# Attention and token-mixing MLP on one core: a new written order for the first two batches, another conversion of the float64 weights, and fp32r in more of group 0's second layer

## The chip, the core and the metric

The kernel runs on one core of a Trainium2 chip. The metric is device time in microseconds (us) of one execution; lower is better. Engines are named as the profile names them: PE is TensorE (matmuls; PEld its weight loads), DVE is VectorE, ACT is ScalarE, POOL is GpSimd, SP issues the DMAs.

## What is computed

Eight batches, eight heads, 576 tokens of 64 values; the attention features are an exponential of a projection, with the largest magnitude of a row taken off. Its output is the input of a block that mixes tokens through two thin matrices and then applies a two-layer MLP. U, V and the two MLP weights come in float64.

```python
def phi(x):
    proj = np.einsum('bhsd,df->bhsf', x, w_phi)
    proj = proj - np.max(np.abs(proj), axis=-1, keepdims=True)
    return np.concatenate([np.exp(proj), np.exp(-proj)], axis=-1)
q_p, k_p = phi(q), phi(k)
kv = np.einsum('bhsf,bhsd->bhfd', k_p, v)
num = np.einsum('bhsf,bhfd->bhsd', q_p, kv)
den = np.einsum('bhsf,bhf->bhs', q_p, np.sum(k_p, axis=2))[..., None] + 1e-06
x = heads side by side of num / den              # (8, 576, 512)
u = x + (x.transpose(0, 2, 1) @ U @ V).transpose(0, 2, 1)
out = u + np.maximum(u @ w_ch1, 0.0) @ w_ch2     # 512 -> 2048 -> 512
```

## The kernel before

**Tiling.** Attention goes by pairs of heads, four pairs a batch. The MLP goes by groups of 512 tokens: a batch gives one group (512 of its 576 tokens), and the 64 tokens left over from each of the eight batches make a ninth. A group takes the 2048 hidden features in 16 tiles f of 128. `hidden(f)` is 12 matmuls of 512 columns into one PSUM bank: the layer-1 weights and the transposed input `uT` are each split into an fp32r high part and a low part, and three of the four products are taken. `relu(f)` moves the result to SBUF, and `add(f)` multiplies it with layer-2 weights into four banks `o`.

**Group 0 is special.** In its `add` the input and the weights are plain fp32: 4 matmuls for a tile (each shows as two records in the trace), with `h` written by one ScalarE `Relu` (L1090) and the converted weight `w_r` used as it is. From group 1 on, `h` is split into `h_hi` (ScalarE, L1095) and `h_lo` (VectorE, L1096) and the weights into `w_hi` and `w_lo`: 12 fp32r matmuls for a tile. The weights of layer 2 are split in `split_w2` (ScalarE L385, VectorE L386), called from group 1's `hidden`.

**Conversion.** `convert` turns a float64 tile (two 32-bit words for a number) into fp32 by integer work: `low` (ScalarE, L227) rounds the low word's upper half, `mask` (VectorE, L231) cuts out the exponent, `size` (ScalarE, L236) rescales it, `shift` is two VectorE instructions (L240, then L243 for the sign bit), and `join` (VectorE, L248) adds the two halves. 32 weight tiles go through it, and four small ones of U and V, which are then rounded and split on VectorE (L292 to L295, L317, L319).

**Order.** The first two batches (`early`) are recorded as numbered steps, each with an engine, and issued in the order of the table `ORDER` written in the file; every engine runs its own steps in that order. A word `*n` puts n filler matmuls on zeros (`busy`) into PE's queue. The table covers the attention of batches 0 and 1, the mixing of batch 0 and the first chunks of group 0's MLP; the parts behind a `/` are issued between the later chunks. From there on a fixed loop (`ordered`) interleaves the MLP of group g with the attention of later pairs.

**Three stages** are used below. Stage 1 runs up to the transposes of batch 0's `u` (L1058), behind which group 0's MLP starts; stage 2 from there to the same transposes of batch 1; stage 3 is one more batch. After it all batches are alike.

Of the kernel before, what the change touches and what calls it, by code (L numbers as in the profile page):

```python
# [1394 lines left out]
```

## Time and profile before

| what | us |
|---|---|
| median of 3 runs | 1145.04 (1143.74 to 1145.18) |
| the profiled execution: its own time | 1143.57 |
| the profiled execution: its span, first to last instruction | 1141.4 |
| PE busy in the span | 1120.8 (98%) |
| VectorE busy in the span | 655.2 (57%) |
| ScalarE busy in the span | 533.2 (47%) |
| stage 1 | 0 to 69.2 |
| stage 2 | 69.2 to 203.3 |
| stage 3 | 203.3 to 330.3 |

The table reads from the top: 98% of the span is PE at work, and the chain of work that ended last is 90% PE, 8% VectorE. Those are averages over stages with different limits, so the stages are read one by one. A PE that is busy in this profile is not always a PE at its peak, since the ends of matmuls are modelled; starts are the safer measure.

### The profile page before, as it was taken

To read this page: it belongs to the slowest core of one execution; us is meant where nothing else is said; L and a number is where in the kernel's file an instruction comes from. 1 tells how busy PE (TensorE), PEld (TensorE's weight loads), DVE (VectorE), ACT (ScalarE), POOL (GpSimd) and SP (SyncE) were. 2 spreads that over 40 slices of the span, in tenths; PEclk is the share of its full clock that TensorE was granted. 3 is DMA by queue.
4 is the path that set the end of the run, shared out by engine and by line. 5 is a ranking of instruction groups with operands and counts; after the bars stand their busy time and mean duration, and the time that the engine had idled before them with its cause. 6 is when DMAs were issued, how large, how long until landed. Compare 5 with 4: busy or idle time off the path is not lost.

```text
span 1141.4 us, 22298 instructions
## 1 busy us (share of the span) xinstructions
PE 1120.8 (98%) x9210; PEld 917.4 (80%) x9217; DVE 655.2 (57%) x1379; ACT 533.2 (47%) x1158; POOL 157.9 (14%) x119
## 2 busy tenths in 40 slices
PE   7889999999999999999999999999999999999998
PEld 5765666688888888888888888888888888888886
DVE  7999988856655656655565655665565633112111
ACT  6888876445534544354534553454544521111110
POOL 4321211011111111011201111111101110000000
PEclk9999999999999999999999999999999999999999
DMA  6355534211122112211131122211121005001001
GB/s 197 88 164 181 167 101 128 103 32 32 52 89 62 32 33 76 88 37 32 51 109 33 32 60 67 75 41 34 58 100 32 20 1 171 1 1 37 1 1 37
DMA packets 90532, 75.73 MB, mean 66 GB/s; under 512 B 51648, under 2 KB 76736, under 8 KB 90304
## 3 DMA queue, kind: packets, MB, share of 16 engines
q1 hardware_dynamic: 90112, 73.79, 21.1%
q8 instruction: 73, 1.20, 0.4%
q10 hardware_dynamic: 320, 0.52, 0.1%
q14 instruction: 27, 0.22, 0.1%
HBM read 55.41 MB, written 18.87 MB: 65 GB/s over the span
## 4 chain that ended last, share of the span: by engine, by line
PE 90%; DVE 8%; DMA 1%; SPq 0%; issue 0%; ACT 0%; DVEq 0%
PE o L1110 35%; PE ph L1079 33%; PE xp L877 5%; PE kv_ps L850 4%; PE pk L810 2%; PE T L732 2%; PE pp L969 1%; PE pt L1058 1%; PE kv_ps L840 1%; PE pq L831 1%; PE pq L832 1%; PE xp L870 1%; PE vp L993 1%; DMA w<-in_moe_w_ch_dram 1%; DVE kp L761 1%; DVE w_r L243 1%
## 5 line engine op out<-in xcount | busy, mean ns | idle before, releaser
L1079 PE MATMUL ph<-uT_hi,w_hi 128*128 128x512 f32 x576 | 231.0, 401 | 0.0
L1096 DVE SCALAR_TENSOR_TENSOR h_lo<-ph,h_hi 128x512 fp32r<-128x512 f32 x128 | 88.4, 690 | 247.4 <-ACT h_hi L1095 247.3
L1079 PE MATMUL ph<-uT_hi,w_lo 128*128 128x512 f32 x576 | 224.9, 390 | 0.0
L1079 PE MATMUL ph<-uT_lo,w_hi 128*128 128x512 f32 x576 | 224.7, 390 | 0.0
L1110 PE MATMUL o<-w_hi,h_hi 128*128 128x512 f32 x512 | 205.4, 401 | 0.0
L1095 ACT ACTIVATE h_hi<-ph 128x512 fp32r<-128x512 f32 x128 | 76.7, 599 | 266.3 <-PE ph L1079 266.2
L1110 PE MATMUL o<-w_lo,h_hi 128*128 128x512 f32 x512 | 200.2, 391 | 0.0
L1110 PE MATMUL o<-w_hi,h_lo 128*128 128x512 f32 x512 | 199.8, 390 | 0.0
L1079 PEld LDWEIGHTS ph<-uT_hi,w_lo 128*128 128x128 f32 x576 | 108.1, 188 | 23.8 <-DVE w_lo L364 0.4
L1079 PEld LDWEIGHTS ph<-uT_hi,w_hi 128*128 128x128 f32 x576 | 108.3, 188 | 22.2 <-issue 0.5
L1079 PEld LDWEIGHTS ph<-uT_lo,w_hi 128*128 128x128 f32 x576 | 108.4, 188 | 21.5 <-issue 1.0
L1110 PEld LDWEIGHTS o<-w_hi,h_lo 128*128 128x128 f32 x512 | 96.1, 188 | 21.1
L1110 PEld LDWEIGHTS o<-w_hi,h_hi 128*128 128x128 f32 x512 | 96.3, 188 | 18.8
L1110 PEld LDWEIGHTS o<-w_lo,h_hi 128*128 128x128 f32 x512 | 96.4, 188 | 17.2
L788 POOL PARTITION_ALL_REDUCE qp_t<-qp_t x24 | 17.8, 741 | 624.1 <-ACT qp_t L787 624.1
L788 POOL PARTITION_ALL_REDUCE qp<-qp x48 | 96.0, 1999 | 32.1 <-ACT qp L787 30.5
L471 DVE TENSOR_TENSOR T<-T,T 64x512 fp32r<-64x512 f32 x96 | 66.2, 689 | 33.4 <-ACT T L468 30.5
L468 ACT CAST T<-T 64x512 fp32r<-64x512 f32 x96 | 55.9, 582 | 28.8 <-PE T L732 15.6
L877 PE MATMUL xp<-kv,qp 128*64 128x65 f32 x2048 | 66.8, 222 | 1.9 <-DVE kv L857 1.5
L877 PEld LDWEIGHTS xp<-kv,qp 128*64 128x64 f32 x2048 | 63.1, 138 | 4.1 <-ACT kp L651 2.0
L850 PE MATMUL kv_ps<-vb,kp 128*64 128x65 f32 x2048 | 65.2, 221 | 0.0
L850 PEld LDWEIGHTS kv_ps<-vb,kp 128*64 128x64 f32 x2048 | 64.2, 138 | 0.0
(158 smaller groups left out, 1567.9 us busy)
## 6 DMA issues: line engine op xcount, KB each, us to landing
w<-in_moe_w_ch_dram SPq DMA_DIRECT2D x32, 512.0 KB, 3.9
raw<-in_q_dram SPq DMA_DIRECT2D x32, 256.0 KB, 2.7
raw<-in_k_dram SPq DMA_DIRECT2D x32, 256.0 KB, 2.9
vb<-in_v_dram SPq DMA_DIRECT2D x64, 128.0 KB, 2.9
u_dram<-x SPq DMA_DIRECT2D x32, 256.0 KB, 2.6
st<-u_dram SPq DMA_DIRECT2D x16, 512.0 KB, 3.8
out_dram<-st SPq DMA_DIRECT2D x32, 256.0 KB, 2.5
t_r<-in_k_dram SPq DMA_DIRECT2D x32, 32.0 KB, 2.1
```

Of the source, the lines that this page charges most:

```text
L243: nc.vector.scalar_tensor_tensor(out=a(), in0=st()[:, :, 1], scalar=-0x80000000, in1=a(), op0=ALU.bitwise_and, op1=ALU.bitwise_or)
L468: nc.scalar.copy(out=dst[0:D], in_=src)
L471: nc.vector.tensor_sub(dst[D:2 * D], src, f32(dst[0:D]))
L732: nc.tensor.transpose(out=pT[:, c * P:(c + 1) * P], in_=self.raw[n][:, c // 2, c % 2, :], identity=ident)
L788: nc.gpsimd.partition_all_reduce(qp[0], qp[1], P, ReduceOp.absmax)
L810: nc.tensor.matmul(pk[:, i, :, :], self.T[0][:, i, cs], w_hl, start=True, stop=True)
L850: nc.tensor.matmul(self.kv_v[z * HP:(z + 1) * HP, f, g, :], kp[f][:, i, z * HP:(z + 1) * HP], self.vb[:, g, t, :], start=False, stop=(t == ...
L877: nc.tensor.matmul(xv[zs, c, :], qp[f][:, c * P + z * HP:c * P + (z + 1) * HP], self.kv[:, f, c // 2, :], start=(f == 0), stop=(f == 1), s ...
L1079: nc.tensor.matmul(ph, l[:, c * P:(c + 1) * P], r[:, c, :], start=(n == 0), stop=(n == len(terms) * NCC - 1))
L1095: nc.scalar.activation(out=h_hi, in_=ph, func=AF.Relu)
L1096: nc.vector.scalar_tensor_tensor(out=h_lo, in0=ph, scalar=0.0, in1=f32(h_hi), op0=ALU.max, op1=ALU.subtract)
L1110: nc.tensor.matmul(self.o[t], l[:, cs], r, start=(f == 0 and n == 0), stop=(f == NFC - 1 and n == len(terms) - 1))
```

## The change

The conversion gets other steps. The upper word is read as fp32 and scaled by 2^-112 on ScalarE (`upper`), then shifted left by 3 as a whole on VectorE (`shift`, one instruction in place); the sign is cut out by `sign`, and `mask`, `size` and the second instruction of `shift` go. For the first eight weight tiles and for U and V the low word is done on VectorE (`low_dve`), otherwise on ScalarE as before. Rounding and copying of U and V move to ScalarE. Group 0's second layer uses the split from its third tile on (f of 2 and more): its weights are split right after conversion, its `h_lo` is made on VectorE, and `add` takes 12 fp32r matmuls instead of 4 fp32 ones. Steps become finer: the largest magnitude of k and its subtraction are two steps, and so are the denominator, its reciprocal and the products. The table `ORDER` is another one (845 numbers in place of 727), with 15 filler matmuls instead of 33.

```diff
-1 4 *8 5o 6 49 2 0 511 3 48 47 515 *1 7a 8 11oo 28ao 31 13 18 32 9o 512 10 46 54a *2 12a 52a
+4 58 1 *8 5o 6 2 *1 7o 8 0 11ao 563 13 28oo 565 32 57 33 18 63a 64 3 9a 10 38 *2 66a 77 55
...
-    def convert(work, st, a, b_, after, n, free):
+    def convert(work, st, a, b_, after, n, free, dve=False):
...
-        def mask():
+        def low_dve():
             nc.vector.tensor_scalar(
-                out=half(1), in0=words()[:, :, 3], scalar1=0x7FF0, scalar2=None,
+                out=b_().bitcast(F32), in0=words()[:, :, 1], scalar1=2.0 ** -13,
+                scalar2=2.0 ** 23, op0=ALU.mult, op1=ALU.add)
+
+        def upper():
+            nc.scalar.activation(
+                out=a().bitcast(F32), in_=st().bitcast(F32)[:, :, 1], func=AF.Copy,
+                scale=2.0 ** -112)
+
+        def sign():
+            nc.vector.tensor_scalar(
+                out=half(1), in0=words()[:, :, 3], scalar1=0x8000, scalar2=None,
                 op0=ALU.bitwise_and)
-
-        def size():
-            nc.scalar.activation(
-                out=half(1), in_=half(1), func=AF.Relu, scale=8.0, bias=e_bias)
 
         def shift():
             nc.vector.tensor_scalar(
-                out=a(), in0=st()[:, :, 1], scalar1=3, scalar2=0x7FFFF8,
-                op0=ALU.logical_shift_left, op1=ALU.bitwise_and)
-            nc.vector.scalar_tensor_tensor(
-                out=a(), in0=st()[:, :, 1], scalar=-0x80000000, in1=a(),
-                op0=ALU.bitwise_and, op1=ALU.bitwise_or)
+                out=a(), in0=a(), scalar1=3, scalar2=None, op0=ALU.logical_shift_left)
...
-            nc.vector.tensor_copy(out=u_all[pr, to, 0, :], in_=u_f[pr, of])
...
+            hi = work.add("ACT", lambda n=n: u_hi(n), (ju, zero), free=(su,))
+            last.append(work.add(
+                "DVE", lambda n=n: u_lo(n), (hi,), free=(su,)))
             for i in (2, 3):
-                nc.vector.tensor_copy(out=u_all[pr, to, i, :], in_=f32(u_all[pr, to, 0, :]))
...
+                last.append(work.add(
+                    "ACT", lambda n=n, i=i: u_copy(n, i), (ju, zero), free=(su,)))
...
-            done.append(work.add("DVE", v_part, (jv,), free=(sv,)))
+            hi = work.add("ACT", v_hi, (jv,), free=(sv,))
+            done.append(work.add("DVE", v_lo, (hi,), free=(sv,)))
...
+            elif f >= LATE:
+                hi = work.add("ACT", lambda f=f: split_w2_hi(f), (j,))
+                j = work.add(
+                    "DVE", lambda f=f: split_w2_lo(f),
+                    (hi, ready[2, f - 1] if f > LATE else None))
...
-                ks = {"t": add("DVE", lambda: k_sub("t"), (Kt,), (s_kt,), (slt,))}
...
+                    km = add(
+                        "DVE", lambda r=r: k_max(r), (Kt if r == "t" else K,),
+                        (s_m, s_kt if r == "t" else s_k[r]))
                     ks[r] = add(
-                        "DVE", lambda r=r: k_sub(r), (K, *([ks[0]] if r else [])),
-                        (s_k[r],), (sls[r],))
+                        "DVE", lambda r=r: k_sub(r), (km,),
+                        free=(s_m, slt if r == "t" else sls[r]))
...
-            if self.g == 1:
-                split_w2(f)
+            if self.g == 1 and f in w_t:
+                split_w2_hi(f)
+                split_w2_lo(f)
...
-            if self.g == 0:
+            if self.g == 0 and f < LATE:
...
-            if self.g == 0:
-                terms = ((terms, w_t[f]),)
+            if self.g == 0 and f < LATE:
+                terms = ((self.h[f], w_t[f]),)
+            else:
+                (h_hi, h_lo), w_hi, w_lo = self.h[f], w_hi_t[2, f], w_lo_t[2, f]
+                terms = ((h_hi, w_hi), (h_hi, w_lo), (h_lo, w_hi))
...
+                if f >= LATE:
+                    s_l[f] = Slot("h_lo")
+                    relu[f] = w.add(
+                        "DVE", (lambda f=f: m.relu_lo(f, got["ph", f])),
+                        (relu[f],), (s_l[f],), (sl,))
```

VectorE in stage 1, where U has been converted (`u_st` is the staged U, `u_all` its rounded copies, `qp` and `kp` features of a pair, `kv` the product of k and v). Before:

```order
L248 ISA u_st<-u_st 128x320
L634 TENSOR_TENSOR qp_0_11_191<-qp_0_11_191,qp_0_10_190 128x512
L290 MEMSET u_all 128x256
L292 CAST u_all<-u_st 128x4x32
L293 TENSOR_TENSOR u_all<-u_st,u_all 128x4x32
L295 CAST u_all<-u_all 128x4x32 x2
L292 CAST u_all<-u_st 64x32
L293 TENSOR_TENSOR u_all<-u_st,u_all 64x32
L295 CAST u_all<-u_all 64x32 x2
```

Of the change, the place where the low parts of U stand on VectorE:

```order
L918 COPY kv_2_745<-kv_ps_2_696 128x260
L233 TENSOR_SCALAR v_st_658<-v_st_658 128x256
L669 TENSOR_TENSOR qp_3_01_664<-qp_3_01_664,qp_3_00_663 128x512
L307 TENSOR_TENSOR u_all<-u_st,u_all 64x32
L307 TENSOR_TENSOR u_all<-u_st,u_all 128x4x32
L1095 TENSOR_TENSOR xs_0_2_739<-x_110,xs_0_2_739 128x256
```

The casts have left VectorE's queue, and the low parts stand among the steps of pairs 2 and 3 instead of pair 0.

VectorE in stage 2, around the weights of tiles 4 to 8 (`w_b` and `w_r` are the two halves of a conversion, `w_lo` a low part). Before:

```order
L240 TENSOR_SCALAR w_r_5_1662<-w_5_1540 128x512
L243 SCALAR_TENSOR_TENSOR w_r_5_1662<-w_5_1540,w_r_5_1662 128x512
L231 TENSOR_SCALAR w_b_7_1671<-w_7_1665 128x512
L248 ISA w_r_3_1557<-w_r_3_1557,w_b_3_1514 128x1024
L248 ISA w_r_4_1560<-w_r_4_1560,w_b_4_1538 128x1024
```

Of the change, ahead of tile 5's `add`:

```order
L248 TENSOR_SCALAR w_r_12_1779<-w_r_12_1779 128x512
L390 TENSOR_TENSOR w_lo_6_1806<-w_r_6_1604,w_hi_6_1801 128x512
L1176 SCALAR_TENSOR_TENSOR h_lo_5_1835<-ph_5_1808,h_hi_5_1821 128x512
L390 TENSOR_TENSOR w_lo_7_1849<-w_r_7_1479,w_hi_7_1847 128x512
L248 TENSOR_SCALAR w_r_8_1706<-w_r_8_1706 128x512
L243 TENSOR_SCALAR w_b_11_1858<-w_11_1764 128x512
L252 ISA w_r_8_1706<-w_r_8_1706,w_b_8_1772 128x1024
L243 TENSOR_SCALAR w_b_6_1856<-w_6_1713 128x512
L421 TENSOR_TENSOR w_lo_5_1875<-w_r_5_1624,w_hi_5_1793 128x512
```

The two-input instruction of the shift is gone; `h_lo` of tile 5 and the low part of its layer-2 weight now stand in the same queue as the conversions of tiles 8 to 12, and tile 5's `add` needs both.

PE in stage 2, the `add` of tile 3 (`o` are the four output banks). Before:

```order
L596 MATMUL pq_1_2_1669<-T_2_1339,w_f 128x512
L601 MATMUL pqt_2_1706<-tail_T_2_1338,w_f 128x128
L1110 MATMUL o_0_1437<-w_r_3_1557,h_3_1609 128x512
L1110 MATMUL o_1_1438<-w_r_3_1557,h_3_1609 128x512
L1110 MATMUL o_2_1439<-w_r_3_1557,h_3_1609 128x512
L1110 MATMUL o_3_1440<-w_r_3_1557,h_3_1609 128x512
```

Of the change, the first bank of the same `add`:

```order
L631 MATMUL pq_1_2_1679<-T_2_1336,w_f 128x512
L1191 MATMUL o_0_1410<-w_hi_3_1645,h_hi_3_1601 128x512
L1191 MATMUL o_0_1410<-w_lo_3_1681,h_hi_3_1601 128x512
L1191 MATMUL o_0_1410<-w_hi_3_1645,h_lo_3_1617 128x512
L1191 MATMUL o_1_1411<-w_hi_3_1645,h_hi_3_1601 128x512
```

Four matmuls with the converted weight became twelve with its two parts; what stands around them is almost the same.

## Rows read from the trace of the kernel before

**Rows 1.** Busy time by stretch: us, then PE, PEld, DVE, ACT, POOL, PEclk, DMA.

```profile
0.00:69.20 69.20, 56.94 (x874) 43.26 (x881) 60.34 (x146) 52.11 (x124) 27.69 (x36) 1.00 0.50 143
69.20:203.30 134.10, 131.37 (x1023) 87.94 (x1023) 120.95 (x247) 106.80 (x203) 22.50 (x14) 0.99 0.48 149
203.30:330.30 127.00, 126.81 (x1091) 105.05 (x1090) 78.44 (x167) 60.95 (x137) 18.74 (x12) 1.00 0.18 55
...
197.30:200.50 3.20, 3.18 (x5) 1.83 (x6) 3.13 (x5) 1.64 (x3) 0.00 (x0) 0.50 0.72 255
```

**Rows 2.** Timeline of VectorE, its first real work: start us, length us, what.

```profile
7.46 0.43 DVE L240 TENSOR_SCALAR w_r<-w 128x512 int32<-128x512 int32 x1 [5.65 <-DMA w<-in_moe_w_ch_dram]
...
8.53 0.68 DVE L759 TENSOR_REDUCE mk<-pk 128x4 f32<-128x512 f32 x1
```

**Rows 3.** Groups by shape, stage 1, VectorE: count | busy us, mean ns | idle before.

```profile
L240 DVE TENSOR_SCALAR w_r<-w 128x512 int32<-128x512 int32 x4 | 3.7, 916 | 5.7 <-DMA w<-in_moe_w_ch_dram 5.6
...
L243 DVE SCALAR_TENSOR_TENSOR w_r<-w,w_r 128x512 int32<-128x512 int32 x4 | 2.8, 694 | 0.1
L317 DVE CAST v_all<-v_st 128x256 fp32r<-128x256 f32 x2 | 2.6, 1319 | 0.0
...
L292 DVE CAST u_all<-u_st 64x32 fp32r<-64x32 f32 x2 | 1.3, 647 | 0.0
```

**Rows 4.** Timelines of VectorE and of GpSimd from 33 to 37 us.

```profile
33.28 1.27 DVE L317 CAST v_all<-v_st 128x256 fp32r<-128x256 f32 x1
...
35.24 1.41 DVE L240 TENSOR_SCALAR w_r<-w 128x512 int32<-128x512 int32 x1
...
33.11 4.22 POOL L630 PARTITION_ALL_REDUCE qp<-qp  x2 [0.17 <-ACT qp L619]
```

**Rows 5.** Groups by shape, stage 2, VectorE, as in Rows 3.

```profile
L248 DVE CUSTOM_DVE_ANT_0 w_r<-w_r,w_b 128x1024 uint16<-128x1024 uint16 x30 | 20.5, 702 | 0.6 <-ACT w_b L236 0.2
L243 DVE SCALAR_TENSOR_TENSOR w_r<-w,w_r 128x512 int32<-128x512 int32 x28 | 20.3, 725 | 0.8
L231 DVE TENSOR_SCALAR w_b<-w 128x512 uint16<-128x512 uint16 x29 | 15.1, 524 | 3.1 <-DMA w<-in_moe_w_ch_dram 3.0
L240 DVE TENSOR_SCALAR w_r<-w 128x512 int32<-128x512 int32 x28 | 12.0, 429 | 0.0
...
L386 DVE TENSOR_TENSOR w_lo<-w_r,w_hi 128x512 fp32r<-128x512 f32 x9 | 6.2, 684 | 0.1
```

**Rows 6.** Page, costliest groups, whole span: the low part of the hidden layer.

```profile
L1096 DVE SCALAR_TENSOR_TENSOR h_lo<-ph,h_hi 128x512 fp32r<-128x512 f32 x128 | 88.4, 690 | 247.4 <-ACT h_hi L1095 247.3
```

**Rows 7.** Groups by shape, stage 2, ScalarE, as in Rows 3.

```profile
L236 ACT ACTIVATE w_b<-w_b,warm 128x512 uint16<-128x512 uint16 x31 | 26.3, 867 | 4.1 <-DVE w_b L231 2.9 <-DVE den L886 1.1
L227 ACT ACTIVATE w_b<-w 128x512 uint16<-128x512 uint16 x28 | 21.3, 781 | 4.5 <-DMA w<-in_moe_w_ch_dram 4.4
L360 ACT CAST w_hi<-w_r 128x512 fp32r<-128x512 f32 x16 | 9.9, 617 | 0.4 <-DVE w_r L248 0.3
```

**Rows 8.** Timeline of PE: two adds in fp32, one in fp32r, and what follows.

```profile
101.37 3.70 PE L1110 MATMUL o<-w_r,h 128*128 128x512 f32 x8
105.00 1.15 PE L877 MATMUL xp<-kv,qp 128*64 128x65 f32 x32
...
187.34 3.59 PE L1110 MATMUL o<-w_r,h 128*128 128x512 f32 x8
190.37 0.68 PE L969 MATMUL pp<-xs,u_all 128*128 128x256 f32 x1
...
278.21 0.40 PE L1110 MATMUL o<-w_hi,h_hi 128*128 128x512 f32 x1
...
280.97 0.60 PE L732 MATMUL T<-ident,raw 128*128 128x128 f32 x4
```

**Rows 9.** Groups by shape, stage 1, PE: the filler matmuls.

```profile
L1164 PE MATMUL busy<-zeros 128*128 128x512 bf16 x26 | 9.7, 467 | 1.4 <-DVE zeros L1159 1.2
```

**Rows 10.** Waits of PE up to 320 us: for whom, us in total, times, longest.

```profile
PE vp L993 <- DVE pst L982: 5.3, 2, 2.9
```

More of the change, by code (lines that the diff above doesn't have):

```diff
@@ L250, in convert @@
         k = n / C
-        p0 = work.add("ACT", low, after, free=free)
-        p1 = work.add("DVE", mask, after, free=free)
-        p2 = work.add("ACT", size, (p1,))
-        p3 = work.add("DVE", shift, after, free=free)
+        if dve:
+            p0 = work.add("DVE", low_dve, after, free=free)
+        else:
+            p0 = work.add("ACT", low, after, free=free)
+        p1 = work.add("ACT", upper, after, free=free)
+        p2 = work.add("DVE", sign, (p0,) if dve else after, free=free)
+        p3 = work.add("DVE", shift, (p1,))
         return work.add("DVE", join, (p0, p2, p3))
@@ L269, in staged @@
         ld = work.add("SP", begin, take=(s,))
-        j = convert(work, lambda: got[0][:, 0:n, :], lambda: part(0), lambda: part(1), (ld,), n, ())
+        j = convert(work, lambda: got[0][:, 0:n, :], lambda: part(0), lambda: part(1), (ld,), n, (), True)
         return j, s, lambda: f32(part(0))
@@ L373, in weight_work @@
                 work, lambda tiles=tiles: tiles["st"], lambda r_=r_: r_().bitcast(I32), b_,
[L374 removed]
+                (ld, *wait), C, (s,), i < 8)
             if m == 1:
@@ L720, in work, with den @@
                 self.G.append(G)
-                self.gp.append(add(
-                    "DVE",
-                    lambda s_=s_: self.out_rest(s_, x_of(), xt0 if s_ == 0 else None),
-                    (G, *slots), free=(sl,)))
+                s_d, tail = Slot("den"), s_ == 0
+                def den(s_=s_, tail=tail):
+                    got["den", s_] = self.out_den(s_, NT + 1 if tail else NT)
+                gd = add("DVE", den, (G,), (s_d,))
+                gi = add("DVE", lambda s_=s_: self.out_inv(got["den", s_]), (gd,))
+                self.gp.append(add(
+                    "DVE", lambda s_=s_: self.out_x(s_, x_of(), got["den", s_]),
+                    (gi, *slots), free=(sl, s_d)))
+                for g in range(2 if tail else 0):
+                    self.gp.append(add(
+                        "DVE", lambda g=g: self.out_xt(g, xt0, got["den", 0]), (gi, *slots),
+                        free=(sl, s_d)))
         def transpose_q(self):
@@ L881, in out_rest, with out_den, out_inv, out_x @@
         def out_rest(self, s, x, xt=None):
-            m = NT if xt is None else NT + 1
-            xv = self.xv[s]
-            den = small.tile([P, 16], F32, tag="den", name=f"den{self.nm}_{s}")[:, 0:m]
-            nc.vector.tensor_scalar_add(den.unsqueeze(2), xv[:, :, D:D + 1], 1e-6)
+            den = self.out_den(s, NT if xt is None else NT + 1)
+            self.out_inv(den)
+            self.out_x(s, x, den)
+            if xt is not None:
+                for g in range(2):
+                    self.out_xt(g, xt, den)
+        def out_den(self, s, m):
+            den = small.tile([P, 8], F32, tag="den", bufs=4, name=f"den{self.nm}_{s}")[:, 0:m]
+            nc.vector.tensor_scalar_add(den.unsqueeze(2), self.xv[s][:, :, D:D + 1], 1e-6)
+            return den
+        def out_inv(self, den):
             nc.vector.reciprocal(out=den, in_=den)
+        def out_x(self, s, x, den):
             xo = x.rearrange("p (z s) c -> p s z c", s=2)[:, s, :, self.h0 * D:(self.h0 + 2) * D]
@@ L1249, in early @@
         chunks = m.chunks()
-        last, relu, s_h, s_o, first = None, {}, {}, [Slot("o") for _ in range(4)], []
+        last, relu, s_h, s_l, s_o, first = None, {}, {}, {}, [Slot("o") for _ in range(4)], []
         for n, (fn, f, *ts) in enumerate(chunks[:CHUNKS]):
```

170 lines of the change are left out of this document (100 added, 70 removed), and 30 rows, old and new, of the table ORDER.

## The prediction, made before the changed kernel was run

> **What bounds the kernel now.** I read the stretches first, because the share of 98% for PE is an average. [rows 1] gives three. In stage 1 (0 to 69.2) PE is busy 56.9 us and VectorE 60.3 us; VectorE's first real work starts at 7.46 [rows 2], so from there to 69.2, 61.7 us, it is busy 98% of the time. Stage 1 ends when VectorE is through. In stage 2 (134.1 us) PE is busy 131.4 us, VectorE 121.0 us (90%) and ScalarE 106.8 us (80%): PE sets the end, with VectorE close behind. In stage 3 PE is busy 126.8 of 127.0 us and VectorE 78.4: PE alone. Behind stage 3 the loop's order is as before, so the time can only change by what the three stages give up. Their waits are few: those for `pst` come to 5.3 us in two places [rows 10], and behind the second the granted clock is 0.50, the 1.2 GHz level, from 197.3 to 200.5 [rows 1].
>
> **Stage 1, what VectorE loses.** The order says what stands ahead of the first low part of `uT`. Weights, before: four shifts of two instructions, 4 x 0.916 + 4 x 0.694 = 6.4 us [rows 3], and three masks at 0.524 [rows 5], 1.6; together 8.0. After: two tiles, each with `shift`, `sign` and `low_dve`, and one more `join` than before. `sign` is the mask with another constant, 0.524. `shift` is L240 without its second operation and without the gaps between words; L240 takes 0.429 where nothing holds it [rows 5], and I take that. `low_dve` reads the same 16-bit words as the mask but writes 32 bits; its nearest rows are 0.429 and 0.725 [rows 5], I take the mask's 0.524. The join is 0.702. That makes 2 x (0.429 + 0.524 + 0.524) + 0.702 = 3.7, so 4.3 us less. The casts of V (2.6 us) and of U (1.3 us for the two that show) go to ScalarE [rows 3]: 3.9 us less. The small conversions of U and V lose an instruction of the shift and gain a low step each, which I put at zero. Sum: 8.2 us less. Against it, the first instruction is now the maximum of k, which stood at 8.53 in place of 7.46 [rows 2]: 1.1 us later. Upper end: 7 us.
>
> The lower end comes from [rows 4]. A cast of V took 1.27 us and a shift 1.41 us, both begun within 0.2 us of the start of an all-reduce on GpSimd (two from 33.11, 4.22 us together). The same L240 takes 0.429 in stage 2. So part of what I took off is not the work of these instructions but a hold-up beside GpSimd, which can pass to the next instruction: 4 x (0.916 - 0.429) = 1.9 for the shifts and, with 0.43 as a cast's own price, 2 x (1.319 - 0.43) = 1.8 for the casts. 7 - 3.7 leaves 3 us.
> The Trainium skill says what that is, in "SBUF — State Buffer", section "SBUF: two separate sides": VectorE and GpSimd share a pair of ports that one instruction holds for its whole length while the other blocks fully. By that rule the hold-up stays as long as the all-reduces stay, and the sum for this stage would be 3; by the durations alone it would be 7.
> I take 6. It is nearer the upper end because the casts of U and V, of the kinds that were caught, leave the queue, and because the maximum and the subtraction of k no longer have to stand back to back. ScalarE covers what it is given: 52.1 us busy in 69.2 [rows 1]. What it gets are 12 small casts, and it gives two `size` steps and two `low` steps of the weights for two `upper` steps. Were that cover gone, the casts would come back on the path at some 0.4 us each.
>
> **Stage 2, PE.** Of the 14 changed `add`s, tiles 2 to 13 are in this stage. An fp32 `add` took 3.63 us from its start to the next matmul's (101.37 to 105.00) or 3.03 (187.34 to 190.37); the fp32r one takes 2.76 (278.21 to 280.97) [rows 8]. The difference is 0.87 or 0.27. In the second case the next matmul starts before the recorded end of the fp32 ones (187.34 + 3.59 = 190.93), so part of the cost is in the follower; I take 0.65, nearer the upper one. 12 x 0.65 = 7.8 us, with ends of 3.2 and 10.4.
>
> **Stage 2, the other engines.** VectorE loses the shift's second instruction (the sign bit) 28 times at 0.725, 20.3 us [rows 5]. It gains: `h_lo` for tiles 2 to 13, 12 x 0.690 = 8.3 [rows 6]; some six more low parts of layer-2 weights than the nine it has now, 6 x 0.684 = 4.1 [rows 5]; two more conversions that stage 1 gave up, 2 x (0.524 + 0.429) = 1.9; `low_dve` for six tiles, 6 x 0.524 = 3.1 (2.6 to 4.4). Net 2.9 less: 118.1 us of work. In a stage of 134.1 - 7.8 = 126.3 us that is 94%; stage 1 shows 98%, so it fits, with little to spare. ScalarE loses 31 `size` steps at 0.867 and gains 30 `upper` steps. None is in the trace: between the cast's 0.617 and the 0.781 of `low`, which reads with the same gaps [rows 7]; I take 0.7. 26.9 - 21.0 = 5.9 less, and four `low` steps (3.1) move off. It ends near 98 us in 126 and covers this.
> The Trainium skill has a price for such a step: "ScalarE: Activation LUTs", section "What ACT_TABLE_LOAD costs", gives 186 ns and 0.833 ns an element without a pointer operand, an estimate of 0.61 us here; by it ScalarE would lose another 2.7 us, none of it on the path.
> The wait for `pst` at the stage's end stays in my sum: the cast and the low part of `pst` stand behind the same exponentials and conversions of tile 15 as before. So stage 2 gives 7.8.
>
> **Stage 3** has tiles 14 and 15: 2 x 0.65 = 1.3 us. The low parts of layer 2 that moved ahead of it were beside PE's work there (VectorE 78.4 of 127.0).
>
> **Sum.** 6 + 7.8 + 1.3 = 15.1 us. The profiled execution took 1143.57, of which 1141.4 is span and 2.2 lies around it and does not change. 1143.57 - 15.1 = 1128.5. That execution lies 1.5 us below the median of the runs; I add about a third of that and say **1129**.
>
> **Rivals.**
> First, **VectorE sets the pace of stage 2 too.** Every changed `add` now waits for a `h_lo` and a weight's low part that stand in a queue filled to 94%. If VectorE keeps its present share of 90%, 118.1 us of work need 131 us, 3.1 less than now, and the sum is 6 + 3.1 + 1.3 = 10.4: 1133. For it: the order gives no slack between the low parts and their `add`. Against it: 98% in stage 1.
> Second, **the finer steps fill the gaps.** Stage 1 gives 9, stage 2 also the wait for `pst` (about 2.4 us of the 5.3) and the 1.6 us lost at half clock: 9 + 7.8 + 4.0 + 1.3 = 22: 1121. For it: PE has 12.3 us free in stage 1. Against it: two engines would have to run above 95% together.
> Third, **the clock falls in stage 1.** Fillers drop from 33 to 15; 26 of them show, 9.7 us [rows 9]. Without them PE's own work there is 47 us of 69. The one stretch at 0.50 came behind a wait for `pst` [rows 1, 10], so gaps do cost clock here. If 30 of the 47 us ran at half, PE would need 77 us, 8 more than the stage has now: 8 - 7.8 - 1.3 = 1 less than now, about 1142.
> The Trainium skill warns of this in "TensorE: Matmul & The Clock Gate", section "Why this matters for your kernels": idle gaps between bursts of matmuls drop the clock to its half rate; by that alone the fillers taken out would cost what I just worked out.
> Fourth, **slower: a weight's DMA holds up the `add`s.** VectorE and ScalarE wait for weight DMAs now and then (3.0 and 4.4 us in stage 2 [rows 5, 7]), and PE doesn't notice, since no `add` of group 0 waits for anything behind them. Now `h_lo` stands in that queue. If each of 14 `add`s waited w, the cost is 14 w; it decides from w = 15.1 / 14 = 1.1 us, and at 2 us each the time is 1128.5 + 28 = 1156.
>
> **Chances.** Forecast 0.50 (1124 to 1132); VectorE as the pace 0.20 (1133); gaps filled 0.17 (1121); clock 0.07 (1142); slower 0.06. The range goes from 1117 (stage 1 at 10, PE at its upper end) to 1139, and leaves out the slower case and most of the clock case. A change of 0.2%, 2.3 us, is about what a measurement of this kernel can tell from none. Faster by more 0.89, within 0.05 (most of the clock case falls here), slower 0.06.
>
> **What would show it.** In the profile after: the transposes of batch 0 near 63 instead of 69; those of batch 1 some 14 us earlier than at 203, and those of batch 2 some 15; 2.76 us for an `add` of tiles 2 to 15; VectorE above 92% in stage 2; the L240-like shift near 0.43 and still some instructions of 1.2 us or more beside an all-reduce. The forecast is wrong if PE waits for `h_lo` or `w_lo` at many `add`s, if the granted clock is 0.50 anywhere between 6 and 60 us, or if stage 1 is no shorter.

## The result, and the profile after

The changed kernel takes 1125.57 us (1125.01 to 1126.18), the kernel before, measured beside it, 1145.08: a ratio of 0.9834 (95% interval 0.9822 to 0.9845), 19.5 us less. The forecast was 1129 with a range of 1117 to 1139. The profiled span fell from 1141.4 to 1123.9, by 17.5 us. That is 2 us less than the medians differ by, because the profiled execution of the kernel before is one of its shorter ones: of 27 executions measured beside the experiments, those with a mean granted clock of 0.997 or 0.998 took 1142.5 to 1143.9 us, like the profiled one, and those with 0.995 or 0.996 took 1144.6 to 1146.8. A stage's end is the first transpose of a batch's u (`pt`):

| | before | after | saved | forecast |
|---|---|---|---|---|
| stage 1 | 69.15 | 60.32 | 8.8 | 6 |
| stage 2 | 134.17 | 127.06 | 7.1 | 7.8 |
| stage 3 | 126.95 | 125.53 | 1.4 | 1.3 |
| behind it | 811.1 | 811.0 | 0.1 | 0 |

Busy time by stretch in the profile after, columns as in [rows 1]: stretch, us, then PE, PEld, DVE, ACT, POOL, granted clock, DMA share, GB/s.

```profile
0.00:60.30 60.30, 53.90 (x863) 42.12 (x863) 50.91 (x129) 49.90 (x129) 27.29 (x35) 1.00 0.53 144
60.30:187.40 127.10, 123.90 (x1070) 97.45 (x1070) 114.62 (x245) 98.34 (x197) 22.36 (x15) 0.99 0.51 163
187.40:312.90 125.50, 125.49 (x1097) 106.47 (x1098) 76.51 (x164) 61.33 (x138) 18.72 (x12) 1.00 0.20 60
148.00:153.00 5.00, 3.50 (x15) 2.35 (x14) 4.81 (x11) 2.35 (x7) 0.00 (x0) 1.00 0.00 0
153.00:156.40 3.40, 3.40 (x10) 2.62 (x9) 3.34 (x9) 2.77 (x6) 0.00 (x0) 0.50 0.00 0
```

VectorE's first real work in the profile after, as in [rows 2]:

```profile
8.64 0.69 DVE L820 TENSOR_REDUCE mk<-pk 128x4 f32<-128x512 f32 x1 [6.83 <-PE pk L643]
```

The bounds are the same as before, each at a lower level. In stage 1 VectorE starts at 8.64 and is busy 50.1 of the 51.7 us that follow, so it still sets the end, with 9.4 us less busy time. In stage 2 PE is busy 123.9 of 127.1 us and VectorE 90%. The stretch at 0.50, the 1.2 GHz level, is still there, but lies at 153 us, behind 5 us in which PE was busy 3.5. What PE waited for, whole stretch up to 320 us (for whom, us in total, times, longest):

```profile
PE vp L1064 <- DVE pst L1053: 1.4, 2, 1.1
...
PE ph L1151 <- DVE h_lo L1176: 0.9, 1, 0.9
```

The waits for `pst`, 5.3 us before [rows 10], are 1.4; in stage 2 alone they fell from 2.4 to 1.1. Of the new low parts only one is ever waited for, once; no `add` of group 0 shows a wait for `w_lo`. VectorE's groups of the conversion in stage 1, then in stage 2, where the same lines are mostly free of GpSimd (as [rows 3] and [rows 5]: count, busy us, mean ns, idle before):

```profile
L252 DVE CUSTOM_DVE_ANT_0 w_r<-w_r,w_b 128x1024 uint16<-128x1024 uint16 x2 | 2.4, 1179 | 0.0
...
L243 DVE TENSOR_SCALAR w_b<-w 128x512 uint16<-128x512 uint16 x2 | 1.6, 822 | 0.0
L248 DVE TENSOR_SCALAR w_r<-w_r 128x512 int32<-128x512 int32 x2 | 1.6, 812 | 0.0
...
L233 DVE TENSOR_SCALAR w_b<-w 128x512 f32<-128x512 uint16 x2 | 1.3, 672 | 0.0
```

```profile
L252 DVE CUSTOM_DVE_ANT_0 w_r<-w_r,w_b 128x1024 uint16<-128x1024 uint16 x29 | 19.7, 690 | 0.4
L243 DVE TENSOR_SCALAR w_b<-w 128x512 uint16<-128x512 uint16 x30 | 16.1, 539 | 3.9 <-DMA w<-in_moe_w_ch_dram 3.8
L248 DVE TENSOR_SCALAR w_r<-w_r 128x512 int32<-128x512 int32 x30 | 14.8, 502 | 2.6 <-ACT w_r L238 2.5
...
L421 DVE TENSOR_TENSOR w_lo<-w_r,w_hi 128x512 fp32r<-128x512 f32 x13 | 9.9, 759 | 1.6 <-ACT w_hi L415 1.4
L1176 DVE SCALAR_TENSOR_TENSOR h_lo<-ph,h_hi 128x512 fp32r<-128x512 f32 x13 | 8.9, 685 | 1.0 <-ACT h_hi L1170 0.9
...
L233 DVE TENSOR_SCALAR w_b<-w 128x512 f32<-128x512 uint16 x6 | 2.5, 410 | 0.0
```

The same join takes 0.69 us in one stage and 1.18 in the other. Timelines of GpSimd and of VectorE from 28 us (start, length) show why:

```profile
28.31 4.18 POOL L665 PARTITION_ALL_REDUCE qp<-qp  x2 [0.62 <-ACT qp L654]
```

```profile
28.34 1.68 DVE L252 CUSTOM_DVE_ANT_0 w_r<-w_r,w_b 128x1024 uint16<-128x1024 uint16 x1
29.94 0.68 DVE L669 TENSOR_TENSOR qp<-qp,qp 128x512 f32<-128x512 f32 x1
30.55 1.27 DVE L243 TENSOR_SCALAR v_st<-v_st 128x256 uint16<-128x256 uint16 x1
```

The two all-reduces each catch the instruction that begins beside their start: a join and a sign step, where before it was a cast and a shift [rows 4].

### The profile page after: what moved, and what is told of

Its sections match the earlier page's. It is cut to its first block, busy times and chain, and to the rows that moved or that the text cites. A ratio compares the mean times of both kernels' runs of the same rounds, so it can differ in the third digit from the quotient of the medians.

```text
span 1123.9 us, 22354 instructions
## 1 busy us (share of the span) xinstructions
PE 1109.1 (99%) x9255; PEld 927.5 (83%) x9255; DVE 637.6 (57%) x1357; ACT 522.6 (47%) x1158; POOL 157.3 (14%) x118
## 4 chain that ended last, share of the span: by engine, by line
PE 92%; DVE 4%; ACT 2%; SPq 1%; DMA 1%; issue 0%; POOL 0%; DVEq 0%; ACTq 0%
PE ph L1151 34%; PE o L1191 34%; PE xp L938 5%; PE kv_ps L911 4%; PE pk L871 2%; PE T L788 2%; PE pt L1129 1%; PE pp L1040 1%; PE kv_ps L901 1%; PE pq L892 1%; PE xp L931 1%; PE pq L893 1%; PE vp L1064 1%; DMA w<-in_moe_w_ch_dram 1%; PE pk L643 0%; PE busy L1245 0%
## 5 line engine op out<-in xcount | busy, mean ns | idle before, releaser
L1176 DVE SCALAR_TENSOR_TENSOR h_lo<-ph,h_hi 128x512 fp32r<-128x512 f32 x142 | 98.0, 690 | 247.9 <-ACT h_hi L1170 247.6
L1191 PE MATMUL o<-w_hi,h_hi 128*128 128x512 f32 x568 | 228.2, 402 | 0.0
L1191 PE MATMUL o<-w_lo,h_hi 128*128 128x512 f32 x568 | 222.2, 391 | 0.0
L1191 PE MATMUL o<-w_hi,h_lo 128*128 128x512 f32 x568 | 221.9, 391 | 0.0
L1170 ACT ACTIVATE h_hi<-ph 128x512 fp32r<-128x512 f32 x142 | 84.9, 598 | 273.7 <-PE ph L1151 273.5
L1191 PEld LDWEIGHTS o<-w_hi,h_lo 128*128 128x128 f32 x568 | 106.7, 188 | 23.3
L1191 PEld LDWEIGHTS o<-w_hi,h_hi 128*128 128x128 f32 x568 | 106.9, 188 | 21.5 <-ACT xs L1090 0.8
L1191 PEld LDWEIGHTS o<-w_lo,h_hi 128*128 128x128 f32 x568 | 107.1, 189 | 19.0
```

The costliest lines, as they stand in the source:

```text
L1170: nc.scalar.activation(out=h_hi, in_=ph, func=AF.Relu)
L1176: nc.vector.scalar_tensor_tensor(out=h_lo, in0=ph, scalar=0.0, in1=f32(h_hi), op0=ALU.max, op1=ALU.subtract)
L1191: nc.tensor.matmul(self.o[t], l[:, cs], r, start=(f == 0 and n == 0), stop=(f == NFC - 1 and n == len(terms) - 1))
```

## The experiments

Every ratio below is against the kernel before; stage lengths are from the profile of each run. The start of stage 1 is not equally early in all of them: VectorE's first real work begins at 8.09 us in the first experiment and at 9.58 in the last but one, and the rest of that stage is the same to 0.5 us there. So a length of stage 1 from one profile is good to about 1 us.

**The additions alone.** In `add`:

```diff
                 terms = ((h_hi, w_hi), (h_hi, w_lo), (h_lo, w_hi))
+                if self.g == 0:
+                    terms = ((f32(h_hi), f32(w_hi)),)
```

> The changed kernel, in its new order, with one edit: the additions of group 0's second layer from the third tile on are single fp32 matmuls again (first factor and first weight parts only, the low parts are still made but not multiplied, so the low terms are left out of the output). Theory A (the gain of stages 2 and 3 is the shorter additions and nothing else): PE's transposes of batch 0's u stay near 60.3 us, stage 2 grows from 127.1 by 12 x 0.63 = 7.5 to about 134.6 (before: 134.2), stage 3 from 125.5 to 126.8, the time to about 1134.5. Rival B (the new order and the finer steps brought it, the additions were covered by waits): stage 2 stays under 130 and the time under 1129.

1132.78 us, ratio 0.9904 (0.9887 to 0.9920). Stretches, then an `add` and its follower on PE in this run:

```profile
59.80:191.80 132.00, 129.61 (x1021) 87.60 (x1022) 116.49 (x247) 99.07 (x199) 22.48 (x15) 1.00 0.51 160
191.80:318.20 126.40, 126.40 (x1090) 105.01 (x1089) 74.86 (x161) 60.72 (x137) 18.74 (x12) 1.00 0.19 56
```

```profile
100.44 3.70 PE L1193 MATMUL o<-w_hi,h_hi 128*128 128x512 f32 x8
104.07 0.66 PE L901 MATMUL kv_ps<-vt,kp_t 128*64 128x130 f32 x8
```

The same `add` in the changed kernel:

```profile
100.32 0.50 PE L1191 MATMUL o<-w_hi,h_hi 128*128 128x512 f32 x1
...
103.28 0.66 PE L901 MATMUL kv_ps<-vt,kp_t 128*64 128x130 f32 x8
```

3.63 against 2.96 us, 0.67 each, and yet stage 2 grows by 5.0, not by 12 x 0.67 = 8.0, and stage 3 by 0.9. Neither theory has it whole. Part of the gap is the clock: this run has no stretch at 0.50, the changed kernel has one that costs 3.4 / 2 = 1.7 us. Of the remaining 1.3 us, 0.8 are PE's waits and gaps (3.2 us in the changed kernel, 2.4 here). The new order with fp32 additions is still 2.1 us shorter in stage 2 than before, but 1.6 of that is the stretch at 0.50 that the kernel before had [rows 1]. At equal clock the order alone is worth 0.5 us in this stage, and the additions 6.7 (5.0 and 1.7), or 6.0 against the run without fillers below, which has no such stretch either.

**VectorE's relief taken back.** In `shift`:

```diff
                 out=a(), in0=a(), scalar1=3, scalar2=None, op0=ALU.logical_shift_left)
+            nc.vector.scalar_tensor_tensor(
+                out=a(), in0=a(), scalar=0, in1=a(), op0=ALU.bitwise_and, op1=ALU.bitwise_or)
```

> The changed kernel with a second VectorE instruction put back into every shift, of the old one's kind and size (a AND 0 OR a, which changes nothing in the result). 30 of them lie in stage 2 and 6 in stage 1. Theory A (VectorE's relief was what made room for the low parts; it has 12.5 us to spare in stage 2): 30 x 0.70 = 21 us more make 135.6 us of VectorE work, more than PE's 123.9, so VectorE sets stage 2 at 95 to 98% busy: 138 to 143 us; stage 1 grows by 2 x 0.70 + 1.4 = 2.8 or more; time about 1141 (1137 to 1145), no better than the kernel before by over 0.8%. Rival B (PE sets stage 2 whatever VectorE does, since its steps can run late): stage 2 stays at 127 to 129, stage 1 plus 1 to 3, time 1127 to 1130.

1149.53 us, ratio 1.0045 (1.0031 to 1.0060): slower than the kernel before, and above theory A's range. Stretches, and PE's longest wait in stage 2:

```profile
0.00:65.00 65.00, 55.27 (x860) 43.54 (x863) 53.75 (x135) 49.79 (x129) 27.90 (x35) 0.97 0.50 136
65.00:208.50 143.50, 128.62 (x1069) 98.64 (x1069) 134.06 (x273) 98.72 (x197) 21.49 (x15) 0.98 0.46 143
```

```profile
PE ph L1153 <- DVE h_lo L1178: 8.3, 6, 2.3
```

Rival B falls. With 134.1 us of work VectorE sets stage 2, and it does so at 93% busy. PE waits for the low part of h, and loses clock besides (0.98 in this stage, 0.97 in stage 1), which theory A had not reckoned with. So in this order the fp32r additions are worth having only with the cheaper conversion. Another order, written for a conversion with that instruction, was not run.

**The casts put back.** In `u_hi`, `u_copy` and `v_hi`:

```diff
-            nc.scalar.copy(
+            nc.vector.tensor_copy(
```

> The changed kernel with the 12 casts of U and V back on VectorE, at the same places of the order. Theory A (VectorE sets stage 1, and each cast it is rid of shortens the stage): the casts came to 6.8 us before, part of it hold-up beside GpSimd; at own prices (0.43, 0.2 and about 0.17 us) they are 2.9. So stage 1 grows by 2.9 to 6.8, to 63.2 to 67.1, and the time to 1128.5 to 1132.4. Rival B (stage 1 became shorter by its order; ScalarE's 49.9 or PE's 53.9 us now set it): stage 1 stays within 1 us of 60.3, time 1125 to 1127.

1128.75 us, ratio 0.9864 (0.9850 to 0.9879).

```profile
0.00:63.20 63.20, 53.66 (x861) 42.12 (x864) 53.98 (x141) 47.56 (x117) 27.49 (x35) 1.00 0.53 146
```

VectorE has 3.1 us more and the stage is 2.8 longer: theory A, at its lower end. The casts cost little more than alone (2.6 us in the kernel before when no all-reduce runs, further down); the hold-up that they showed before hardly comes back with them.

**No fillers.** In `Work.issue`:

```diff
-                self.keep_busy(int(word[1:]))
+                self.keep_busy(0)
```

> The changed kernel without any of the filler matmuls of stage 1. Theory A (VectorE sets stage 1 and the clock holds by the real work): granted clock 1.00 from 6 to 60 us as now, stage 1 within 0.5 us of 60.3, time 1125 to 1127. Rival C (the fillers hold the clock): a stretch at 0.50 shows between 6 and 60 us, PE's 53 us grow past 60, stage 1 takes 4 to 8 us more and the time is 1130 to 1134.

1124.77 us, ratio 0.9832 (0.9817 to 0.9847), not to be told from the changed kernel.

```profile
6.00:59.90 53.90, 47.99 (x841) 38.82 (x839) 50.10 (x126) 47.49 (x126) 25.48 (x19) 1.00 0.53 143
59.90:185.90 126.00, 122.78 (x1069) 96.16 (x1069) 114.59 (x245) 98.18 (x197) 22.36 (x15) 1.00 0.52 164
152.00:156.00 4.00, 4.00 (x19) 3.12 (x19) 3.91 (x8) 3.33 (x7) 0.00 (x0) 1.00 0.00 2
```

Rival C falls: 48.0 us of real work in 53.9 keep the granted clock at 1.00. PE's wait of 0.9 us for `h_lo` is there as in the changed kernel, but this time no stretch at 0.50 follows, and stage 2 is 1.1 us shorter. Why it follows in one execution and not in the other stays open.

**The cheaper conversion in the old order.** The kernel before, in `shift`:

```diff
-            nc.vector.scalar_tensor_tensor(
-                out=a(), in0=st()[:, :, 1], scalar=-0x80000000, in1=a(),
-                op0=ALU.bitwise_and, op1=ALU.bitwise_or)
```

> The kernel before, in its old order, with the second VectorE instruction of every shift taken out (the words lose their sign, which the output then lacks). It does alone what the change does to VectorE's conversions. Theory A (VectorE sets stage 1, PE sets stage 2): stage 1 loses up to 4 x 0.69 + 1.4 = 4.2 us and at least half of it, to 65 to 67 us; stage 2 gives only what its waits for pst and the stretch at 0.50 hold, 0 to 3 of 134.2; time 1139 to 1143. Rival B (VectorE's 121 us also hold up stage 2 here): stage 2 falls by 4 us or more, time under 1138.

1138.73 us, ratio 0.9946 (0.9929 to 0.9962).

```profile
0.00:65.40 65.40, 55.63 (x873) 42.79 (x880) 56.14 (x138) 52.05 (x124) 27.33 (x36) 1.00 0.54 150
65.40:198.00 132.60, 129.39 (x1027) 87.46 (x1024) 102.56 (x219) 105.66 (x204) 20.54 (x14) 1.00 0.49 150
```

Theory A, its time 0.3 us under the range: stage 1 gives 3.7 us for 4.1 us of VectorE's work. Stage 2 gives 1.6, the stretch at 0.50, although VectorE loses 18.4 us there: PE sets that stage.

**All-reduces replaced by a DMA**, in the changed kernel and in the kernel before, in `q_max`:

```diff
-                nc.gpsimd.partition_all_reduce(qp[0], qp[1], P, ReduceOp.absmax)
+                nc.scalar.dma_start(out=qp[0], in_=qp[1])
```

> The changed kernel with GpSimd's all-reduce over the partitions replaced by a DMA copy of the same tile, issued by ScalarE, in the first two batches (the maximum over the partitions is left out: each value stands for itself). The wait for the result stays, GpSimd's work goes. Theory A (VectorE instructions that begin beside an all-reduce are held up by it): the eight instructions of stage 1 above 0.85 us lose together 5.8 us against their own prices; VectorE's 50.9 us fall to about 45 and stage 1 to 55 to 57, where PE's 53.9 us come next; time 1120 to 1123. Rival D (they are slow for another reason, or the hold-up is hidden by waits): still instructions of 1.2 us or more, stage 1 within 1 us of 60.3, time 1125 to 1127.

> The kernel before with the same edit: a DMA copy issued by ScalarE in place of each all-reduce of the first two batches (the maximum over the partitions is left out). Theory A: the ten instructions of stage 1 above 0.8 us lose together about 8 us, the casts of V and the shifts come down to about 0.43 us, VectorE's 60.3 us fall to about 52 and stage 1 to 61 to 63. With the run of the changed kernel without all-reduces this prices stage 1 of both without the hold-up: the difference of the two stages is then the work alone, 6 to 7 us, against 8.8 with it. Rival D: stage 1 within 1 us of 69.2.

1150.78 us (1.0047, 1.0031 to 1.0063) and 1159.59 us (1.0138, 1.0107 to 1.0169). The stages and the times can't decide between the theories: VectorE waited up to 9.0 us for the DMA, and stage 1 grew to 76.1 and 78.0. The single instructions can. Of the changed kernel so edited, stage 1, VectorE:

```profile
L252 DVE CUSTOM_DVE_ANT_0 w_r<-w_r,w_b 128x1024 uint16<-128x1024 uint16 x2 | 1.4, 681 | 0.0
...
L243 DVE TENSOR_SCALAR w_b<-w 128x512 uint16<-128x512 uint16 x2 | 0.9, 460 | 0.0
L248 DVE TENSOR_SCALAR w_r<-w_r 128x512 int32<-128x512 int32 x2 | 0.8, 420 | 0.0
```

And of the kernel before so edited:

```profile
L240 DVE TENSOR_SCALAR w_r<-w 128x512 int32<-128x512 int32 x4 | 1.7, 421 | 5.7 <-DMA w<-in_moe_w_ch_dram 5.7
...
L317 DVE CAST v_all<-v_st 128x256 fp32r<-128x256 f32 x2 | 0.8, 391 | 0.0
```

The casts of V fall from 1.319 [rows 3] to 0.391, the shifts from 0.916 to 0.421. VectorE's busy time falls by 5.9 us in the one and by 7.4 in the other, as expected of a hold-up beside GpSimd.

**The maximum left out**, so that there is neither an all-reduce nor a wait; again in both kernels:

```diff
-                nc.gpsimd.partition_all_reduce(qp[0], qp[1], P, ReduceOp.absmax)
+                pass
...
-                nc.vector.tensor_sub(qp[1], qp[1], qp[0])
+                nc.vector.tensor_sub(qp[1], qp[1], qp[1])
```

> The changed kernel with the maximum over the partitions left out of the first two batches: no all-reduce on GpSimd and no wait for one; the subtraction on VectorE, of the same shape, takes the tile from itself. The DMA copy of the run before showed VectorE's busy time in stage 1 at 45.0 us instead of 50.9, but brought waits of up to 9 us that spoilt the stage. Theory A (the hold-up beside the all-reduces costs stage 1 of the changed kernel 5 to 6 us): no VectorE instruction above 0.85 us in stage 1, VectorE near 45 us, stage 1 between 54.5 (PE has 53.9 us of work) and 57, time 1119 to 1122. Rival D (what is held lies beside waits that stay): stage 1 within 1.5 us of 60.3, time 1124 to 1127.

> The kernel before with the maximum over the partitions left out of the first two batches in the same way: no all-reduce, no wait for one. In the changed kernel this took 6.4 us off VectorE's work in stage 1 and 3.4 off the stage (60.3 to 56.9). Theory A (part of the 8.8 us that stage 1 gained is less hold-up): VectorE's 60.3 us fall to about 52.5, stage 1 by more than 3.4 us, to 61.5 to 65; without hold-up the two kernels' stages then lie 4.6 to 8 us apart. Rival F (the gain is work and order alone, the hold-up passed on whole): stage 1 falls by 3.4 or less, to 65.8 to 69, and the stages stay 8.8 us or more apart.

1119.08 us (0.9773, 0.9756 to 0.9791) and 1135.28 us (0.9916, 0.9898 to 0.9934). Stage 1 of the changed kernel, then of the kernel before:

```profile
0.00:56.90 56.90, 53.00 (x861) 42.02 (x864) 44.50 (x129) 49.12 (x128) 3.12 (x20) 1.00 0.56 150
```

```profile
0.00:62.90 62.90, 57.09 (x881) 43.21 (x881) 52.59 (x146) 51.94 (x124) 3.12 (x21) 1.00 0.56 157
```

The changed kernel loses 3.4 us of stage 1, the kernel before 6.3, each as its theory A said. Without the all-reduces the two stages lie 6.0 us apart, with them 8.8. But a stage's length is not the size of the hold-up. VectorE's busy time falls by 6.4 us in the changed kernel (50.9 to 44.5) and by 7.7 in the kernel before (60.3 to 52.6). The changed kernel can't use all of its 6.4: there VectorE is then busy only 43.7 of the 48.2 us from its first real work on, and PE, with 53.0 of 56.9, comes next. So of the 9.4 us of busy time that the change took off VectorE in stage 1, 1.3 are hold-up and 8.1 other work. Rival F falls by its numbers, though most of the hold-up, 6.4 of 7.7 us, was passed on as it says.

**The finer steps put together again.** `den` and `inv` do nothing, the step of the first product issues all, and the maximum of k stands at its subtraction:

```diff
-                gd = add("DVE", den, (G,), (s_d,))
-                gi = add("DVE", lambda s_=s_: self.out_inv(got["den", s_]), (gd,))
+                gd = add("DVE", lambda: None, (G,), (s_d,))
+                gi = add("DVE", lambda: None, (gd,))
...
-                    "DVE", lambda s_=s_: self.out_x(s_, x_of(), got["den", s_]),
+                    "DVE", rest,
```

> The changed kernel with the finer steps put together again: denominator, reciprocal and the products issued in one piece at the place of the first product, and the maximum of k in one piece with its subtraction at the place of the latter. Same instructions, same order of the rest. Theory A (the steps' splitting moves little; VectorE's sum sets stage 1): stage 1 within 1 us of 60.3, stage 2 within 1 of 127.1, time 1125 to 1127. Rival E (the finer steps fill VectorE's and PE's gaps, which is where the 2.8 us came from that stage 1 gained beyond the forecast): stage 1 grows by 2 to 4 us, time 1128 to 1130.

1130.65 us, ratio 0.9873 (0.9858 to 0.9888): 5.1 us more than the changed kernel.

```profile
0.00:64.00 64.00, 55.63 (x861) 43.86 (x864) 52.34 (x129) 49.75 (x129) 26.92 (x35) 0.97 0.52 142
64.00:193.00 129.00, 123.76 (x1070) 96.53 (x1070) 116.88 (x245) 98.60 (x197) 22.48 (x15) 1.00 0.50 157
31.80:37.50 5.70, 4.12 (x77) 3.83 (x75) 4.97 (x11) 4.34 (x12) 1.12 (x2) 0.71 0.38 91
```

Rival E: stage 1 grows by 3.7 us and stage 2 by 1.9, or by 3.0 against the run without fillers, which has no stretch at 0.50 in stage 2 either. In stage 1 a stretch at 0.50 is part of it: behind a wait of PE of 1.6 us for `kv` the granted clock is 0.71 on average over the 5.7 us of the last row. The order was written for the finer steps, so this is the most they can bring; an order written for the joined ones might lose less.

**Two attempts at a faster version.** Without fillers and with two words of the order swapped, so that `h_lo` of tile 10 goes ahead of a weight's low part; then also with the low steps of U, V and the first two weights on ScalarE:

```diff
-533 517 529 744 840 718 ...
+533 517 529 840 744 718 ...
```

> An attempt at a faster version. The changed kernel without fillers (1124.8 in the run above) and with two neighbours of the order swapped: the low part of h of tile 10 goes ahead of a weight's low part (step 840 ahead of 744), since PE waited 0.94 us for it at 151.9 before the stretch at 0.50. Theory A: that wait falls to about 0.3, no stretch at 0.50, stage 2 at 125.3 to 125.8, time 1123.5 to 1124.6. Rival: the wait moves to the next thing in VectorE's queue, stage 2 at 126 or more, time 1124.5 to 1126.

```diff
-        j = convert(... lambda: part(1), (ld,), n, (), True)
+        j = convert(... lambda: part(1), (ld,), n, ())
...
-                (ld, *wait), C, (s,), i < 8)
+                (ld, *wait), C, (s,), 2 <= i < 8)
```

> As the kernel with the two neighbours swapped, and with the low steps of U, V and the first two weights on ScalarE in place of VectorE (2 x 0.67 and 1.27 us off VectorE, some 2.6 us on ScalarE, which has 49.9 of 60.3). Theory A (VectorE's work sets stage 1): stage 1 falls by 1.5 to 2.6 us to 57.3 to 58.4, time 1121 to 1123. Rival: the steps stand behind ScalarE's copies and exponentials and VectorE waits for them, or GpSimd's hold-up passes on: stage 1 within 0.5 us of 59.9 or longer, time 1124 or more.

1124.68 us (0.9822, 0.9806 to 0.9837) and 1124.28 us (0.9820, 0.9804 to 0.9836): neither can be told from the changed kernel. The swap did what it was to do, the wait for `h_lo` is 0.3 us, but a wait of 0.6 us for a low part of the weights came up behind it, and stage 2 is 125.8, where it was 126.0 without the swap. Stage 1 came out at 60.8, since VectorE's first real work began at 9.58 in this execution. The low steps are the telling case. Stretch and VectorE's groups in stage 1:

```profile
0.00:59.90 59.90, 50.38 (x849) 40.73 (x849) 50.49 (x124) 51.55 (x134) 26.76 (x35) 1.00 0.54 145
```

```profile
L669 DVE TENSOR_TENSOR qp<-qp,qp 128x512 f32<-128x512 f32 x8 | 7.2, 916 | 0.1
L669 DVE TENSOR_TENSOR qp_t<-qp_t 128x128 f32<-128x128 f32 x5 | 3.0, 602 | 0.2 <-POOL qp_t L665 0.2
...
L252 DVE CUSTOM_DVE_ANT_0 w_r<-w_r,w_b 128x1024 uint16<-128x1024 uint16 x2 | 1.3, 683 | 0.0
```

Five instructions are gone (x124 for x129), not six: only one of the two weights has its low step in stage 1. They took 1.9 us in the changed kernel, 1.4 at the prices of the run without the maximum. VectorE's busy time is 50.5 instead of 50.9. The join is free now (683 ns); the subtractions of q, 704 ns in the changed kernel, are held in its place (916). Against those same prices the instructions of stage 1 are held by 7.4 us together in the changed kernel and by 7.7 here. Theory A falls: hold-up of 0.5 us left with the five steps, 0.8 came back on others, and the rest of what left the queue shows as less overlap between neighbours.

## Why the prediction was right, and where its sizes were off

**Stage 1, 6 forecast, 8.8 measured.** The mechanism held: VectorE sets the stage, and what left its queue shortened it. Three sizes were wrong. The casts were summed from the two groups that stood out, 3.9 us; the trace of the kernel before has four more groups of them, two of which are

```profile
L317 DVE CAST v_all<-v_st 128x64 fp32r<-128x64 f32 x1 | 1.2, 1185 | 0.0
L295 DVE CAST u_all<-u_all 64x32 fp32r<-64x32 f32 x4 | 1.1, 506 | 0.0
```

and together they are 6.8, of which 2.6 are left when no all-reduce runs. The conversion of the weights, 4.3 us less by prices from stage 2, gave only 1.5: before, 3.7 + 2.8 + 1.4 + 0.7 = 8.5 us; after, 2.4 + 1.6 + 1.6 + 1.3 = 7.0, because the all-reduces now catch these steps. (In the two runs without the maximum it is 6.5 and 4.0.) That these two errors nearly cancel is luck. Two additions to x (2 x 0.68) also fall behind the stage's end now. The later start came as forecast (8.64).

The allowance for hold-up was the third: of 3.7 us that I knew as hold-up I let 1 pass on. In VectorE's busy time, by the pair of runs without the maximum, hold-up is 7.7 us before and 6.4 after: 1.3 went, and most was passed on. The bound of 3 us, by which all that was known of it stays, was too low all the same, because it counts 8.2 - 3.7 = 4.5 us of other work where 8.1 went: 2.6 of casts, 2.6 of weights, the two additions, and a rest of small conversions and closer overlap that no run separates. So the stage adds up as 8.1 of work, 1.3 of hold-up and 0.6 of VectorE's idle time (2.2 us before, 1.6 after), less the later start of 1.2: 8.8.

The Trainium skill's rule behind that bound ("SBUF — State Buffer", "SBUF: two separate sides") is narrower than the prediction has it: on VectorE's side it names instructions with two SBUF inputs or in a mode that uses two ports, not every instruction. The traces agree in that instructions that read PE's output are not held (last section), and in that with the all-reduces gone no instruction of the stage is held. Of the rule's length they show less: beside two all-reduces of 4.18 us the join took 1.0 us more, the subtraction behind it took its usual 0.68, and the sign step took 1.0 more.

The rival of filled gaps, put at 9 us for this stage, had more to it than I gave it: put together, the steps cost up to 3.7 us here, part of it at the lower clock.

**Stage 2, 7.8 forecast, 7.1 measured.** PE does set it, and VectorE has room: 90%, not 94%. The groups that the forecast summed fell from 74.1 to 71.9 us, by 2.2 (2.9 forecast), all instructions together by 4.0; the busy time fell by 6.4, since it counts the overlap of neighbours once. An `add` differs by 0.67 us in the same place of the same order, 0.65 was taken. Where the next matmul comes early, part of that is in the followers, as I argued: at tile 5 it starts 0.31 us sooner and the group behind it 0.73. Of the 8.0 us that twelve such `add`s make, the stage got 6.0 to 6.7 at equal clock, and 0.5 from its order, which I had put at nothing. The term's size was a little too high, and the order makes up for part of it. That the wait for `pst` would stay was wrong, 1.1 of 2.4 us are left; what I had coupled to it, 3.2 us at half clock, stayed in size (3.4) at another place, behind waits for `tail_T` and `h_lo`, so that it takes the same from both kernels.

**VectorE as the pace.** It didn't happen, but was closer than 0.20 may read. I argued that 94% fits because stage 1 runs at 98%. That share was misread: it counts 0.8 us of memsets ahead of 7.46, and without them it is 59.5 of 61.7 us, 96%. With the second shift back, stage 2 did not get above 93%. At that share the 118.1 us forecast would have needed 118.1 / 0.93 = 127 us, the stage as it is.

**Stage 3, 1.3 forecast, 1.4 measured**; 0.9 of it is the two additions, the other 0.5 is there with fp32 additions too and no run shows its source. That the number fits is partly luck.

**Prices.** `sign` 0.539 and join 0.690 came as taken (0.524, 0.702); `shift` 0.502 (0.429 taken, it is that where no all-reduce runs: 0.418 to 0.420), `low_dve` 0.410 (0.524). `upper` on ScalarE is

```profile
L238 ACT ACTIVATE w_r<-w 128x512 f32<-128x512 f32 x30 | 19.4, 672 | 2.2 <-DMA w<-in_moe_w_ch_dram 2.2
```

It takes 0.672 where 0.7 was taken. By the Trainium skill's price ("ScalarE: Activation LUTs", "What ACT_TABLE_LOAD costs") it was an estimate of 0.61; the trace decides, and nothing on the path depends on it.

**The other rivals.** The clock in stage 1 is 1.00 with 15 fillers and with none. The Trainium skill's warning ("TensorE: Matmul & The Clock Gate", "Why this matters for your kernels") fits the run with joined steps in kind: behind a wait of 1.6 us 0.71 on average, so at the lower level for a part, over 5.7 us in which PE was busy 4.1. The slower case, a weight's DMA ahead of `h_lo`, needed 1.1 us at every `add`; VectorE did wait 3.8 us for weights in stage 2, and PE waited once for `h_lo`, 0.9 us.

**Signs.** The transposes of batch 0, 1 and 2 stand at 60.3, 187.4 and 312.9: 8.8, 15.9 and 17.4 us earlier, where 6, 14 and 15 were named. An `add` of tiles 2 to 13 takes 2.72 to 2.96 us (2.76 named) where PE doesn't wait behind it. VectorE above 92% in stage 2 did not come (90%). Some instructions of 1.2 us or more are still there beside an all-reduce.

**The time.** Of the 3.4 us between 1129 and 1125.57, 2.4 come from the stages, 0.4 from the time around the span (2.2 taken, 1.8 now), and the rest mostly from what I added for the median.

## What to carry to other kernels

Where two engines share a stage, work taken off one pays only up to the other's bound: in the old order 18.4 us less work for VectorE gave 1.6 in stage 2. Here a cheaper conversion made room on VectorE and shorter matmuls used it; with one instruction of the conversion put back, the same order was slower than the kernel before. An instruction that a neighbour engine holds up should be priced where nothing holds it, and the hold-up priced by itself, by a run without the neighbour. Read it in the busy time of the engine that is held, since the stage can run into another bound. Most of it goes to whatever stands there next. Sum a kind of instruction over all its shapes, since the small ones were as long as the large ones here.

## What the runs showed of the hardware beside that

In stage 1 of the two kernels, 18 VectorE instructions began within 0.4 us of the start of an all-reduce of some 2 us (1.9 to 2.4). Twelve of them took 0.7 to 1.0 us longer than without all-reduces, whatever their own length (a 64-column cast 1.185 for 0.194, a join 1.68 for 0.69), and ended 1.2 to 1.7 us behind that start. All twelve work from SBUF to SBUF. Five that read PE's output took their usual time, as did one reciprocal of five numbers a row. An example is the maximum of k in [rows 2], 0.68 us from 8.53 on, beside this one of the kernel before:

```profile
8.29 2.12 POOL L630 PARTITION_ALL_REDUCE qp<-qp  x1 [4.80 <-ACT qp L619]
```

So what stands beside the start of an all-reduce decides what it costs; no run here tried an order made for that. The instruction behind a held one was held too in some cases, by 0.6 us, and not in others.

A DMA copy of a tile from SBUF to SBUF, in place of an all-reduce, made VectorE wait up to 9.0 us in stage 1, where the weights' loads are under way; an all-reduce takes 2.

The granted clock fell to 0.50 behind 1.4 us of waits in one kernel, none longer than 0.9, and stayed at 1.00 behind the same waits in another.
